# Halved second expert product in steps 5 to 15 of a fused attention and expert kernel

## The chip, the cores and the metric

The kernel runs on one core of a Trainium2 chip. The metric is the device time of one execution in microseconds. A core has TensorE (matrix products into PSUM; the trace calls its matmuls PE and its weight loads PEld), VectorE (DVE), ScalarE (ACT), GpSimd (POOL), and SyncE (SP), whose queue issues all DMA transfers of this kernel. Each engine works through its own queue in order and waits there for what its next instruction needs.

## The reference

The reference is chunked attention over 4 sequences of 768 tokens with 8 heads of 64, whose output x (3072 tokens by 512) goes through four experts, every token through all of them:

```
p = domain_probs / (domain_probs.sum(-1) + 1e-9)
for e in range(4):
    h = maximum(x @ w1[e], 0)          # 512 -> 1024
    out += p[:, e:e+1] * (h @ w2[e])   # 1024 -> 512
```

All inputs and the output are float32.

## The kernel before

**Precision.** Every operand of a large product is split into a high part and a low part (each of the type fp32r); a product is hi x hi + hi x lo + lo x hi, three matmuls accumulated in PSUM. `two_parts` (L306 ScalarE copy, L307 subtraction) makes such a pair; `split` (L344, L348) does it for single blocks of w1 and w2.

**Steps.** The expert part is a sequence of 16 steps n = 0 to 15: batch n // 4 (768 tokens, two halves of SG = 384), expert n % 4. Step 0 is computed plainly in the first block with attention of the first batch. From step 1 on, the first product (x @ w1) is done by seven products of half matrices in place of eight. Its blocks of w1 come in 4 pairs (block p and p + 4); per pair the sums S1 to S4 of weight blocks are formed, and the class `Pair` runs the seven products, 42 matmuls of 384 columns (`product`, L511), with results combined through PSUM and a small tile u (L524 copy, L528 addition) and then `relu` (L449, L450). The input side needs sums too, which `combine_x` makes once per batch (L317 to L326) into xa, xb and xc.

**Second product.** `Second` computes one tile of 128 tokens by 512 columns: 8 blocks of w2, three matmuls of 512 columns each (L482), 24 per tile, six tiles per step. The result times the routing weight is added into an SBUF tile acc (L496; L494 for the first expert), and stored after the fourth expert (L498). The very last tile is done as two halves of 256 columns.

**Weights.** In steps 1 to 4, `prep_pair` makes the w1 sums for a pair on POOL (L397 to L400) in the scratch tile s_t, of which there is one, splits them into four tiles of w1pool (8 buffers, two pairs) with L306/L307, and stores those in DRAM (`keep`, L359). In steps 0 to 3, `prep2` loads w2 blocks into the tile raw (3 buffers), splits them into w2pool (8 buffers) and stores them likewise. Later steps load the finished parts from DRAM (`again`, L363).

**Order.** TensorE's order is as written (`manual_schedule` for PE). The order on the other engines and on SP's queue is made by the planner of the framework, which plays the program through in a simulation and gives a buffer to the next ready user, by place in the program. Attention of later batches is spread over the steps in windows (`attend`), up to step 11: about two units of 96 queries per step.

**Last lines.** In step n, `tail`, the last tile of step n - 1, runs within pair 0 of step n; `next_pair` prepares pairs 2 and 3 of the step during pairs 1 and 2, and the first two pairs of step n + 1 during the second product.

Of the kernel before, what the change touches and what calls it, by code (L numbers as in the profile page):

```python
# [59 lines left out]
def tile_chunked_attention_moe(ctx: ExitStack, tc: tile.TileContext, qk, v, probs, w1, w2, out):  # L60
# [6 lines left out]
    raw = ctx.enter_context(tc.tile_pool(name="raw", bufs=3))  # L67
    w1pool = ctx.enter_context(tc.tile_pool(name="w1pool", bufs=8))
    w2pool = ctx.enter_context(tc.tile_pool(name="w2pool", bufs=8))
    hpool = ctx.enter_context(tc.tile_pool(name="hpool", bufs=NF * 2))  # L70
    opool = ctx.enter_context(tc.tile_pool(name="opool", bufs=6))
    dram = ctx.enter_context(tc.tile_pool(name="dram", bufs=1, space=DRAM))
# [7 lines left out]
    def open_late():  # L80
        head_ctx.close()
        late["sb"] = ctx.enter_context(tc.tile_pool(name="late", bufs=1, reuse_waits="tile"))
        late["s"] = ctx.enter_context(tc.tile_pool(name="ps_s", bufs=1, space=PSUM))
        late["a"] = ctx.enter_context(tc.tile_pool(name="ps_a", bufs=2, space=PSUM))
        late["xc"] = tuple(
            late["sb"].tile([P, 6, SG], F32R, name=f"xc_{part}", bufs=1) for part in ("hi", "lo")
        )

    idle = const.tile([P, P], mybir.dt.bfloat16, name="idle")
# [13 lines left out]
    ident = const.tile([P, P], F32, name="ident")  # L103
# [153 lines left out]
    def mix(u):  # L257
# [17 lines left out]
    xa, xb = (  # L275
        tuple(const.tile([P, NC, SG], F32R, name=f"{name}_{part}") for part in ("hi", "lo"))
        for name in ("xa", "xb")
# [31 lines left out]
    def combine_x(first):  # L309
# [4 lines left out]
        xc_hi, xc_lo = late["xc"]  # L314
        t3 = late["sb"].tile([P, NC, 256], F32, name="s_t").rearrange("p a b -> p (a b)")[:, 0:h2 * SG]
        t3 = t3.rearrange("p (a b) -> p a b", a=h2)
# [22 lines left out]
    def split(which, n, f):  # L339
# [7 lines left out]
        def low(eng):  # L347
            eng.tensor_tensor(out=lo, in0=r, in1=hi.bitcast(F32), op=ALU.subtract)  # L348
            if which == 2:
                keep(t, (2, n % E, f))  # L350
# [3 lines left out]

    kept = {}

    def keep(t, key, width=DM):
# [3 lines left out]
    def again(pool, name, key, width=DM):  # L361
        t = pool.tile([P, 2, DM], F32R, name=name)
        nc.sync.dma_start(t.bitcast(F32)[:, :, 0:width], kept[key])  # L363
        return t

    def prep2(n, f):
        if n >= E * B or (2, n, f) in wt:
            return
        if n < E:
            fetch(2, n, f)  # L370
            split(2, n, f)(nc.gpsimd)
        else:
            t = again(w2pool, "w2", (2, n % E, f))
            wt[2, n, f] = t[:, 0, :], t[:, 1, :]

# [9 lines left out]
    def prep_pair(n, p):  # L385

        if n >= E * B:
            return
        q = DM // 2
        if n > E:  # L390
            g = [again(w1pool, "w1", (1, n % E, p, i), DM if i < 3 else q) for i in range(4)]
        else:
            r = wp[n, p]
            a21, a22, a11, a12 = (r[:, i, :] for i in range(4))
            t = late["sb"].tile([P, 4, 256], F32, name="s_t")
            s4, s1, s2, s3 = (t[:, i, :] for i in range(4))
            nc.gpsimd.tensor_tensor(out=s1, in0=a21, in1=a22, op=ALU.add)  # L397
            nc.gpsimd.tensor_tensor(out=s2, in0=s1, in1=a11, op=ALU.subtract)
            nc.gpsimd.tensor_tensor(out=s4, in0=a12, in1=s2, op=ALU.subtract)
            nc.gpsimd.tensor_tensor(out=s3, in0=a11, in1=a21, op=ALU.subtract)  # L400
            g = [w1pool.tile([P, 2, DM], F32R, name="w1") for _ in range(4)]

            def put(i, lo, hi, x):
                two_parts(g[i][:, 0, lo:hi], g[i][:, 1, lo:hi], x, nc.vector)

            put(0, 0, DM, r[:, 2:4, :].rearrange("p a b -> p (a b)"))
            put(1, 0, q, a22)
# [356 lines left out]
```

## Time and profile before

| | |
|---|---|
| Time, median of 3 runs | 1114.11 us (1113.42 to 1116.62) |
| Profiled execution | 1114.95 us, span 1113.2 us |
| TensorE matmul busy | 1090.0 us, 6248 matmuls |
| VectorE, ScalarE, POOL busy | 589.6, 439.2, 161.8 us |
| Mean DMA rate | 204 GB/s over the span |
| Granted TensorE clock | 0.995 |

Rows of the profile read as follows. A group row names line, engine, operation, output <- inputs, shape and count, then after the bar busy time and mean ns of one, then idle time of the engine ahead of it and what ended that. A row of the timeline begins with start and duration in us; brackets hold the idle time before it and what ended it. The chain of waits follows the work that ended last. In the stage view each engine's busy time stands for a stretch of the span.

### The profile page before, as it was taken

To read this page: it belongs to the slowest core of one execution; us is meant where nothing else is said; L and a number is where in the kernel's file an instruction comes from. 1 tells how busy PE (TensorE), PEld (TensorE's weight loads), DVE (VectorE), ACT (ScalarE), POOL (GpSimd) and SP (SyncE) were. 2 spreads that over 40 slices of the span, in tenths; PEclk is the share of its full clock that TensorE was granted. 3 is DMA by queue.
4 is the path that set the end of the run, shared out by engine and by line. 5 is a ranking of instruction groups with operands and counts; after the bars stand their busy time and mean duration, and the time that the engine had idled before them with its cause. 6 is when DMAs were issued, how large, how long until landed. Compare 5 with 4: busy or idle time off the path is not lost.

```text
span 1113.2 us, 16383 instructions
## 1 busy us (share of the span) xinstructions
PE 1090.0 (98%) x6248; PEld 974.3 (88%) x6248; DVE 589.6 (53%) x1033; ACT 439.2 (39%) x919; POOL 161.8 (15%) x147
## 2 busy tenths in 40 slices
PE   7999999999999999999999999999999999999998
PEld 6888878988889898898989889898898989899897
DVE  6847985858775444445655534544474403233241
ACT  6555853637444343342523433332351313122130
POOL 4536531615241000000030000000012000000000
PEclk8999999999999999999999999999999999999999
DMA  7645882937379183571938538193652908264431
GB/s 241 226 149 201 321 311 95 403 147 287 146 273 348 62 319 124 216 251 66 338 107 302 182 136 297 62 335 108 241 201 107 338 29 328 88 260 155 163 122 57
DMA packets 87022, 226.57 MB, mean 204 GB/s; under 512 B 11552, under 2 KB 27168, under 8 KB 86944
## 3 DMA queue, kind: packets, MB, share of 16 engines
q1 hardware_dynamic: 86944, 225.53, 56.0%
q8 instruction: 49, 0.80, 0.3%
q14 instruction: 29, 0.24, 0.1%
HBM read 173.06 MB, written 52.43 MB: 203 GB/s over the span
## 4 chain that ended last, share of the span: by engine, by line
PE 84%; DVE 6%; issue 3%; ACT 2%; DMA 2%; POOL 2%; SPq 0%; DVEq 0%; ACTq 0%; POOLq 0%
PE moe_ps L482 43%; PE a_ps L511 20%; PE moe_ps L511 14%; PE moe_ps L439 2%; PE s_ps L147 2%; PE x_ps L263 2%; DMA k<-w 1%; DVE w L307 1%; DVE band L208 1%; ACT s_sb L164 1%; DVE aT L252 1%; DVE u L528 0%; ACT w L306 0%; DVE sm L195 0%; DVE s_sb L187 0%
## 5 line engine op out<-in xcount | busy, mean ns | idle before, releaser
L482 PE MATMUL moe_ps<-w,h_hi 128*128 128x512 f32 (+1 forms) x1552 | 478.8, 390 | 1.1 <-DVE h_lo L450 1.1
L482 PEld LDWEIGHTS moe_ps<-w,h_hi 128*128 128x128 f32 x1552 | 287.8, 188 | 60.3 <-DVE h_lo L450 1.4
L482 PE MATMUL moe_ps<-w,h_lo 128*128 128x512 f32 (+1 forms) x776 | 301.5, 389 | 0.0
L482 PEld LDWEIGHTS moe_ps<-w,h_lo 128*128 128x128 f32 x776 | 145.7, 188 | 30.0
L449 ACT ACTIVATE h_hi<-u 128x384 fp32r<-128x384 f32 x180 | 94.5, 525 | 173.5 <-DVE u L528 173.4
L496 DVE SCALAR_TENSOR_TENSOR acc<-moe_ps,pr,acc 128x512 f32<-128x512 f32 (+1 forms) x73 | 54.2, 742 | 156.3 <-PE moe_ps L482 155.7
L450 DVE SCALAR_TENSOR_TENSOR h_lo<-u,h_hi 128x384 fp32r<-128x384 f32 x180 | 106.9, 595 | 44.3 <-ACT h_hi L449 39.8
L528 DVE TENSOR_TENSOR u<-moe_ps,u 128x384 f32<-128x384 f32 x120 | 66.8, 556 | 106.2 <-PE moe_ps L511 105.7
L511 PE MATMUL a_ps<-xc_hi,w 128*128 128x384 f32 x480 | 104.6, 339 | 2.7 <-ACT u L524 2.0
L524 ACT COPY u<-a_ps 128x384 f32<-128x384 f32 x120 | 57.4, 478 | 106.0 <-PE a_ps L511 103.6
L511 PEld LDWEIGHTS a_ps<-xc_hi,w 128*128 128x128 f32 x480 | 86.3, 189 | 6.6 <-ACT u L524 3.5
L252 DVE STREAM_TRANSPOSE aT<-band 32x256 f32<-32x256 f32 x192 | 83.3, 434 | 10.2 <-ACT band L217 7.9
L164 ACT COPY s_sb<-s_ps 96x64 f32<-96x64 f32 (+1 forms) x96 | 39.6, 438 | 81.4 <-PE s_ps L147 80.8
L511 PE MATMUL a_ps<-xc_lo,w 128*128 128x384 f32 x240 | 61.6, 337 | 0.0
L450 DVE SCALAR_TENSOR_TENSOR h_lo<-a_ps,h_hi 128x384 fp32r<-128x384 f32 x60 | 33.1, 552 | 53.0 <-ACT h_hi L449 53.0
L511 PE MATMUL a_ps<-xb_hi,w 128*128 128x384 f32 x240 | 53.0, 343 | 5.6 <-DVE u L528 5.5
L348 POOL TENSOR_TENSOR w<-raw,w 128x512 fp32r<-128x512 f32 x31 | 43.8, 1422 | 82.1 <-ACT w L344 79.4
L528 DVE TENSOR_TENSOR u<-a_ps,u 128x384 f32<-128x384 f32 x60 | 33.4, 556 | 40.8 <-PE a_ps L511 23.3
L175 POOL MEMSET s_sb<- 32x64 f32 x4 | 0.6, 145 | 364.0 <-DVE acc L496 364.0
L511 PE MATMUL a_ps<-xa_hi,w 128*128 128x384 f32 x240 | 52.6, 341 | 0.3 <-DVE h_lo L450 0.3
L511 PE MATMUL moe_ps<-xb_hi,w 128*128 128x384 f32 x240 | 52.0, 339 | 0.0
L511 PE MATMUL moe_ps<-xa_hi,w 128*128 128x384 f32 x240 | 51.9, 338 | 0.0
(114 smaller groups left out, 1424.7 us busy)
## 6 DMA issues: line engine op xcount, KB each, us to landing
w<-k SPq DMA_DIRECT2D x228, 512.0 KB, 6.2
k<-w SPq DMA_DIRECT2D x80, 512.0 KB, 5.6
w<-k SPq DMA_DIRECT2D x44, 256.0 KB, 4.8
qk_t<-in_qk_dram SPq DMA_DIRECT2D x24, 448.0 KB, 3.5
raw<-in_w_dram SPq DMA_DIRECT2D x32, 256.0 KB, 5.1
v_t<-in_v_dram SPq DMA_DIRECT2D x32, 256.0 KB, 3.3
raw_pair<-in_w_dram SPq DMA_DIRECT2D x32, 256.0 KB, 4.7
out_dram<-acc SPq DMA_DIRECT2D x23, 256.0 KB, 2.0
```

The source lines that it names most:

```text
L147: nc.tensor.matmul(s_ps[0:UQ, j * NPAIR + g, :], lhsT=st[u]["qk"][rows, g * UQ:(g + 1) * UQ], rhs=st[u]["qk"][rows, NPAIR * UQ + g * P:NPA ...
L164: nc.scalar.copy(s_sb[rows, :, dst], s_ps[rows, :, src])
L252: nc.vector.transpose(out=aT[kb * CH:(kb + 1) * CH, :, c * CH:(c + 1) * CH], in_=band[c * CH:(c + 1) * CH, :, kb * CH:(kb + 1) * CH],)
L263: nc.tensor.matmul(x_ps[j * D:(j + 1) * D, g, :], lhsT=v_t[:, h * D:(h + 1) * D], rhs=aT[:, j * NPAIR + g, :], start=True, stop=True,)
L348: eng.tensor_tensor(out=lo, in0=r, in1=hi.bitcast(F32), op=ALU.subtract)
L449: last["act"] = nc.scalar.activation(h_hi[:, lo:hi], ps[:, lo:hi], AF.Relu)
L450: last["dve"] = nc.vector.scalar_tensor_tensor(out=h_lo[:, lo:hi], in0=ps[:, lo:hi], scalar=0.0, in1=h_hi.bitcast(F32)[:, lo:hi], op0=ALU. ...
L482: nc.tensor.matmul(self.ps, lhsT=h[:, self.rows], rhs=w[:, cols], start=(i == 0 and k == 0), stop=(i == NF - 1 and k == 2),)
L496: nc.vector.scalar_tensor_tensor(out=o, in0=self.ps, scalar=p_e, in1=o, op0=ALU.mult, op1=ALU.add)
L511: nc.tensor.matmul(ps, lhsT=w[:, c * P:(c + 1) * P], rhs=y[:, k0 + c, :], start=(first and i == 0), stop=(i == len(steps) - 1), skip_group ...
L524: nc.scalar.copy(u, ps)
L528: nc.vector.tensor_tensor(out=u, in0=ps, in1=u, op=ALU.add)
```

## The change

From step 5 to step 15 the second product too is done by seven products of halves: the hidden values h are split into halves by tokens (384) and by hidden columns (512), w2 by hidden rows (512) and output columns (256). Each of the seven products takes, for each of three token tiles, 4 blocks times 3 matmuls of 256 columns. Results accumulate in the two column halves of a PSUM bank per token tile and are added into acc after every product.

The weight sums T1 to T4 are made once per expert in steps 1 to 4 by the new function `prep2_combined`, called after each pair's `prep2`, from the raw blocks p and p + 4 (in step 4, expert 0, they are fetched again). It uses s_t and a new tile t_hi with one buffer, and stores four pieces of 256 KB per call. From step 5 all weights come from DRAM through one ring of 8 buffers (`Stream`), in the order of use. The sums of hidden values are made on POOL or VectorE and split (`Full.sums`, `split`). The pools of steps 1 to 4 are closed before step 5 and a new pool takes their place; xc moves to the constant pool, idle and ident to the pool of the first block, and the DMA scratch size is halved.

```diff
+    def open_fin():
+        mid_ctx.close()
+        late["sb"] = late["fin"] = ctx.enter_context(tc.tile_pool(name="fin", bufs=1, reuse_waits="tile"))
...
+    def prep2_combined(n, p):
+
+        e, q = n % E, DM // 2
+        if n >= E:
+            for f in (p, p + NH):
+                fetch(2, n + E * B, f)
+                raws[n, f] = wt[2, n + E * B, f]
+        r0, r1 = raws[n, p], raws[n, p + NH]
+        b11, b12, b21, b22 = r0[:, 0:q], r0[:, q:], r1[:, 0:q], r1[:, q:]
+        t = late["sb"].tile([P, 4, 256], F32, name="s_t")
+        t1, t2, t3, t4 = (t[:, i, :] for i in range(4))
+        nc.gpsimd.tensor_tensor(out=t1, in0=b12, in1=b11, op=ALU.subtract)
+        nc.gpsimd.tensor_tensor(out=t2, in0=t1, in1=b22, op=ALU.subtract)
+        nc.gpsimd.tensor_tensor(out=t4, in0=b21, in1=t2, op=ALU.add)
+        nc.gpsimd.tensor_tensor(out=t3, in0=b22, in1=b12, op=ALU.subtract)
+        for i in range(2):
+            x = t[:, 2 * i:2 * i + 2, :].rearrange("p a b -> p (a b)")
+            hi = late["sb"].tile([P, DM], F32R, name="t_hi")
+            nc.scalar.copy(hi, x)
+            (nc.gpsimd, nc.vector)[i].tensor_tensor(
+                out=x.bitcast(F32R), in0=x, in1=hi.bitcast(F32), op=ALU.subtract
+            )
+            k = kept2("t2", e, i)
+            nc.sync.dma_start(k[:, p, 0], hi.bitcast(F32))
+            nc.sync.dma_start(k[:, p, 1], x)
...
+    class Stream:
...
+        def send(self):
+            q = DM // 2
+            while self.sent < min(len(self.keys), self.free + self.RING):
+                key = n, which, x, i = self.keys[self.sent]
+                t = late["fin"].tile([P, 2 * DM], F32R, name="ring", bufs=self.RING)
...
+                    src = kept2(kind, n % E, half)[:, 2 * i:2 * i + 2, :, o * q:(o + 1) * q]
+                nc.sync.dma_start(dst.bitcast(F32), src)
...
+        def sums(self):
+
+            eng = nc.vector if self.p == NP2 - 1 else nc.gpsimd
+            s1, s2 = self.new("s1"), self.new("s2")
+            eng.tensor_tensor(out=s1, in0=self.u22, in1=self.u21, op=ALU.add)
+            eng.tensor_tensor(out=s2, in0=self.u11, in1=s1, op=ALU.subtract)
+            self.split("S2", s2)
+            self.split("S1", s1)
+            nc.gpsimd.tensor_tensor(out=self.u21, in0=self.u11, in1=self.u21, op=ALU.subtract)
+            self.split("S3", self.u21)
+            nc.gpsimd.tensor_tensor(out=self.u12, in0=self.u12, in1=s2, op=ALU.add)
+            self.split("S4", self.u12)
...
+        def go(self, name, t):
+            left, right = self.WITH[name]
...
+            for k in range(NP2):
+                w = self.stream.at[self.n, 2, right, k // 2][:, k % 2]
+                hi, lo = self.k[k][left]
+                for i, (x, y) in enumerate(((hi, 0), (hi, 1), (lo, 0))):
+                    nc.tensor.matmul(
+                        ps, lhsT=x[:, rows], rhs=w[:, y, :],
+                        start=(begins and k == 0 and i == 0), stop=(k == NP2 - 1 and i == 2),
...
+                nc.vector.scalar_tensor_tensor(out=o, in0=ps, scalar=p_e, in1=o, op0=ALU.mult, op1=ALU.add)
...
-        for n in range(1, B * E):
+        for n in range(1, E + 1):
...
             for f in KORDER[0:2]:
                 prep2(n, f)
+            prep2_combined(n, 0)
             pair.seven()
...
                 for f in KORDER[2 * p:2 * p + 2]:
                     prep2(n, f)
+                prep2_combined(n, p)
                 if p + 1 < NP2:
                     next_pair(n, p + 1)
...
         tail.go()
+        open_fin()
+        us, i = windows[E + 1, "A"]
+        load_qk(us[i])
+
+        stream = Stream(range(E + 1, B * E))
...
+            second.go("1", 0)
+            pair.four()
+            pair.three()
+            pair.sums()
+            second.go("1", 1)
+            second.go("2", 0)
+            second.go("2", 1)
+            second.go("1", 2)
+            second.go("2", 2)
...
+            for name in "65":
+                for t in range(NTT):
+                    second.go(name, t)
+            attend(n, "B")
+            for name, t in (("7", 2), ("7", 0), ("7", 1), ("4", 2), ("4", 0), ("4", 1), ("3", 0), ("3", 2)):
+                second.go(name, t)
...
-    nc = _bacc.Bacc("TRN2", target_bir_lowering=False, num_devices=1, dynamic_dma_scratch_size=1024)
+    nc = _bacc.Bacc("TRN2", target_bir_lowering=False, num_devices=1, dynamic_dma_scratch_size=512)
```

More of the change, by code (lines that the diff above doesn't have):

```diff
@@ L385, in prep_pair @@
     def prep_pair(n, p):
[L387 removed]
+        if n > E:
             return
         q = DM // 2
[L390 to L407, printed above, removed]
[L408 to L412 removed]
@@ L631, in window @@
             scores(u)
-            if u + 1 < len(units):
+            if not last and u + 1 < len(units):
                 load_qk(u + 1)
```

238 lines of the change are left out of this document (201 added, 37 removed).

## The prediction

> **What bounds the kernel now.** I read the page first, for the share of each engine.
>
> ```profile
> span 1113.2 us, 16383 instructions
> ...
> PE 1090.0 (98%) x6248; PEld 974.3 (88%) x6248; DVE 589.6 (53%) x1033; ACT 439.2 (39%) x919; POOL 161.8 (15%) x147
> ```
>
> TensorE is busy nearly all the time and sets the end. The profiled execution took 1114.95 us, of which 1113.2 us are the span; the sum is made against 1114.95, which is 0.84 us above the median of the three timed runs. Then the chain of waits in order of time (start, duration, what), at some marks. L482 x18 begins where the first product of a step ends.
>
> ```profile
> 217.53 4.12 PE moe_ps L482 x18
> 355.88 4.12 PE moe_ps L482 x18
> 1012.52 4.12 PE moe_ps L482 x18
> 1018.73 23.16 PE moe_ps L482 x102
> 1066.38 2.11 PE a_ps L511 x12
> 1074.79 4.12 PE moe_ps L482 x18
> ```
>
> A late step without attention takes 1074.79 - 1012.52 = 62.27 us. A 512-column matmul costs 23.16 / 102 = 227 ns, a 384-column one 2.11 / 12 = 176 ns; 168 x 0.176 + 144 x 0.227 = 62.3 us, so the late steps are pure TensorE, with nothing in between. There a shorter product is worth its full time.
>
> **The product itself.** The changed steps run 7 x 3 x 12 = 252 matmuls of 256 columns in place of 144 of 512. The last output tile of the kernel before is computed in two halves of 256 columns, so the price is in the trace: TensorE in order of time near the end, where each such row is followed by one h_lo matmul; below them the group of their weight loads, for later.
>
> ```profile
> 1104.00 0.40 PE L482 MATMUL moe_ps<-w,h_hi 128*128 128x256 f32 x2
> ...
> 1108.67 0.40 PE L482 MATMUL moe_ps<-w,h_hi 128*128 128x256 f32 x2
> ...
> L482 PEld LDWEIGHTS moe_ps<-w,h_hi 128*128 128x128 f32 x1552 | 287.8, 188 | 60.3 <-DVE h_lo L450 1.4
> ```
>
> Thirteen groups of three in 4.67 us are 120 ns per matmul. 252 x 0.120 = 30.2 us against 144 x 0.227 = 32.7 us: 2.4 us less per step, 11 steps: **-26.4 us**. [...]
>
> **What the changed steps need beside TensorE.** First the weights. Per step the ring brings 7.34 MB for each product, 14.7 MB in about 60 us: 246 GB/s. The second product's pieces have runs of 1 KB. Two stretches of the DMA view, one with packets of 4 KB alone, one (2 us at 474) with mostly 1 KB packets by number, and the page's landing time of the stored weights:
>
> ```profile
> DMA packets 567, 2.06 MB, mean 413 GB/s; under 512 B 63, under 2 KB 63, under 8 KB 567
> DMA packets 410, 0.78 MB, mean 390 GB/s; under 512 B 29, under 2 KB 283, under 8 KB 410
> ...
> w<-k SPq DMA_DIRECT2D x228, 512.0 KB, 6.2
> ```
>
> In the second, about 127 packets of 4 KB account for 127 x 4 KB x 16 / 413 GB/s = 20 us of the 32 engine-us; the 254 of 1 KB share 12 us, 47 ns each, about 345 GB/s. So 7.34 / 0.413 + 7.34 / 0.345 = 39 us of transfer hide in a step of 60. A ring slot is reloaded at least one pair (42 x 0.176 = 7.4 us of TensorE) before its use, against 6.2 us: hidden, with little to spare.
>
> Then VectorE and ScalarE. Stage view over one step's length with two attention units and over one without (columns: stretch, length, PE, PEld, DVE, ACT and POOL busy, clock, DMA share, GB/s), and the prices of the new small operations:
>
> ```profile
> 422.28:488.68 66.40, 66.40 (x377) 59.55 (x377) 32.53 (x62) 22.65 (x49) 0.00 (x0) 1.00 0.55 196
> 950.26:1012.52 62.26, 62.26 (x313) 56.48 (x313) 19.54 (x34) 13.49 (x29) 0.00 (x0) 1.00 0.52 185
> L496 DVE SCALAR_TENSOR_TENSOR acc<-moe_ps,pr,acc 128x256 f32<-128x256 f32 x2 | 1.0, 485 | 4.5 <-PE moe_ps L482 4.5
> L528 DVE TENSOR_TENSOR u<-moe_ps,u 128x384 f32<-128x384 f32 x120 | 66.8, 556 | 106.2 <-PE moe_ps L511 105.7
> ```
>
> VectorE per step: 21 evictions x 0.485, and 42 operations of 384 columns (12 adds, 28 low parts, two sums) x 0.556, together 33.5 us in place of 19.5. Two attention units add 32.5 - 19.5 = 13 us: 46.5 of 64 us. The steps that also combine the inputs of the next batch (7 and 11) are fuller still. TensorE waits only where an eviction comes late; the shortest cover is one piece of 12 matmuls, 1.44 us, against 0.485. I put 3 us on all eleven steps (below: 0; above: 10, if step 7 and 11 queue up). ScalarE rises to about 40 of 64 us, POOL to 15. The end: one eviction and one 256 KB store in place of halves, +0.3 us.
>
> **The preparation in steps 1 to 4** is where I expect the time to go. The T weights are made by a new function, 16 calls, 4 per step. A call takes the scratch tile s_t, of which there is one, and the new tile t_hi, also one. s_t is today used by the preparation of the first product's weights (prep_pair, L397 to L400). POOL and DVE in order of time show how it is passed on:
>
> ```profile
> 126.44 0.74 POOL L397 TENSOR_TENSOR s_t<-raw_pair 128x256 f32<-128x256 f32 x1 [1.95 <-issue]
> 157.16 0.73 POOL L397 TENSOR_TENSOR s_t<-raw_pair 128x256 f32<-128x256 f32 x1 [3.31 <-issue]
> 197.31 1.04 DVE L307 TENSOR_TENSOR w<-s_t,w 128x256 fp32r<-128x256 f32 x1
> 198.49 0.94 POOL L397 TENSOR_TENSOR s_t<-raw_pair 128x256 f32<-128x256 f32 x1 [0.41 <-POOL w L348]
> 206.76 0.74 POOL L397 TENSOR_TENSOR s_t<-raw_pair 128x256 f32<-128x256 f32 x1 [3.56 <-issue]
> 315.52 0.73 POOL L397 TENSOR_TENSOR s_t<-raw_pair 128x256 f32<-128x256 f32 x1 [3.76 <-DVE w L307]
> 319.76 0.74 POOL L397 TENSOR_TENSOR s_t<-raw_pair 128x256 f32<-128x256 f32 x1 [1.31 <-DVE w L307]
> ```
>
> The next use starts 0.14 us after the last reader ends (198.35 to 198.49): s_t is always in somebody's hands, partly because a preparation waits, holding it, for weight buffers (157 to 198). The preparations of pairs 2 and 3 run about 8 us ahead of the TensorE that uses them: the one at 198.49 is for pair 3 of step 2, whose S2 is needed 4.2 us before 217.53. There is no slack for more. An unhindered hold is 319.76 - 315.52 = 4.2 us, with queues 8.3 (198.49 to 206.76); I take 6.5.
>
> One call of the new function holds s_t until its last store has left it, and between its two halves t_hi must be stored too: two POOL operations, ScalarE copy, store, ScalarE copy, VectorE subtraction, store. Prices: POOL from the view of s_t, the rest from the groups by shape.
>
> ```profile
> L398 POOL TENSOR_TENSOR s_t<-s_t,raw_pair x16: 727/740/1202, 82.2 to 338.7; 128x256 f32<-128x256 f32 x16
> L344 ACT CAST w<-raw 128x512 fp32r<-128x512 f32 x32 | 19.7, 618 | 5.8 <-DMA raw<-in_w_dram 5.2
> L307 DVE TENSOR_TENSOR w<-s_t,w 128x512 fp32r<-128x512 f32 x16 | 13.7, 858 | 2.9 <-ACT w L306 2.9
> ```
>
> 2 x 0.74 + 2 x 0.62 + 0.86 = 3.6 us, five handovers of 0.15 and half a us of queueing (an estimate): 4.8 us, plus two stores of 256 KB. How long these take depends on the load. The stage view with POOL alone (length, POOL, clock, DMA share, GB/s), the landing times of 256 KB in 186 to 228 and in 409 to 475, and on the page:
>
> ```profile
> 150.00:186.00 36.00, 7.46 (x8) 1.00 0.38 137
> 186.00:228.00 42.00, 25.41 (x24) 1.00 0.94 365
> ...
> raw<-in_w_dram SPq DMA_DIRECT2D x8, 256.0 KB, 5.0
> ...
> v_t<-in_v_dram SPq DMA_DIRECT2D x2, 256.0 KB, 3.2
> ...
> out_dram<-acc SPq DMA_DIRECT2D x23, 256.0 KB, 2.0
> ```
>
> The DMA engines are already full in the first product of step 2, just where calls fall; the change adds 16 stores of 256 KB, 4.2 MB, to each of the four steps. A store lies between 2.0 us (quiet) and 5.0 (full). I take 3.6, the middle, since a step that grows longer has less load per us. One call is then c = 4.8 + 2 x 3.6 = **12 us**; bounds 8.8 and 14.8. [...]
>
> Now the chain of s_t. The calls stand before the preparations of pairs 2 and 3 in the program, so I expect the planner to serve them first when both are ready. From 126 us, where the fourth preparation starts, to the end of the last one lie 13 preparations (84 us), 15 calls (15c), one combination of inputs (8 us), and about 8 us in which a preparation waits for weight buffers: 126 + 84 + 15c + 16. The S2 part of the last is ready 2.5 us before its end, and TensorE wants it at 355.88 - 4.2 = 351.7. The stall over steps 1 to 4 is 15c - 128, nothing below c = 8.5: **+52 us** at c = 12. Late behind it are the raw tiles of w2 (three buffers, now held through the call), and whatever SP queues behind a store that waits.
>
> Other edits at nothing: the unchanged first product's matmuls, moved pools and scratch size; the ring's first loads, whose buffers are free from the middle of step 4, 30 us before use. Sum: 1114.95 - 26.4 + 3 + 0.3 + 52 = 1143.9, **1143 us** beside the median.
>
> **Rivals.** (1) The scratch tile is hidden: the calls go into the quiet stretches (150 to 186: DMA share 0.38, POOL 7.5 of 36 us) and the stores take 2 us, c at or under 8.5. For it: seven tenths of the DMA time there is free; against: s_t is held by a waiting preparation in just these stretches. Time 1114.1 - 26.4 + 3.3 = 1091. (2) Stores at the full load's 5.0 us: c = 14.8, stall 94, 1185. Against: once TensorE stalls, the load thins out. (3) The stall equals the gain at c = 10.1; 0.2 us of c is 3 us, so no change is a narrow case. (4) The halves do not go faster since a weight load (188 ns in its group) bounds a short matmul: 252 x 0.188 = 47 us per step, +160 us; the 120 ns row speaks against it, 1 in 50. (5) VectorE or the ring bounds the changed steps: 2.4 us of each is given back, near 1114 with the preparation hidden; the bounds above leave it unlikely.
>
> **How the numbers follow.** Chain as summed, c from 10.3 to 14.8, that is 1118 to 1185: 0.50, with the likeliest near 1143. Beyond: 0.07. Hidden or half hidden (1087 to 1110): 0.37. Between, within 0.3% (3.3 us, about what a measurement of this kernel can tell from no change): 0.06. The range to 8 in 10 takes both signs, 1087 to 1187; the likeliest case alone spans 1118 to 1185. Faster 0.37, same 0.06, slower 0.57.
>
> **What would show it.** The period of the last steps should be near 59.8 us, with 120 ns per matmul of 256. The first x18-like mark of step 4 (355.88 now) should come some 50 us later, with TensorE waiting for L306/L307 parts of s_t and stores from s_t and t_hi of 3 to 4 us. The prediction is wrong if step 4's first product ends near 356 us, if the holds of s_t by the new function are under 9 us, or if the planner serves pairs 2 and 3 first and TensorE never waits for them.

## The result and the profile after

The changed kernel takes 1215.62 us (median of 4 runs, 1213.58 to 1216.68) against 1114.42 us of the kernel before beside it: a ratio of 1.0903, 95% interval 1.0881 to 1.0925, 101 us slower. The forecast was 29 us slower; the time lies above the whole range.

The page of the kernel after, its span and engines:

```profile
span 1214.2 us, 19938 instructions
PE 1088.4 (90%) x7412; PEld 1023.6 (84%) x7412; DVE 783.3 (65%) x1355; ACT 595.0 (49%) x1271; POOL 403.3 (33%) x381
```

TensorE is as long busy as before (1088 against 1090 us); what was added to the span is waiting. The waits of TensorE, after (waiting product and line, what it waited for, us in total, times, longest):

```profile
PE a_ps L553 <- ACT w L308: 57.4, 8, 11.8
PE a_ps L553 <- ACT u L674: 36.8, 22, 4.8
```

Two waits hold nearly all of it, one in each part of the kernel. L308 is the split of the w1 sums out of s_t in steps 1 to 4 (L306 before). L674 is in the new code of steps 5 to 15. The chain of waits, after, at the ends of the first products of steps 1, 2 and 4, and for steps 14 and 15 at the same place of each (some 36 matmuls into the second product):

```profile
164.00 4.12 PE moe_ps L524 x18
250.18 4.12 PE moe_ps L524 x18
427.45 4.12 PE moe_ps L524 x18
...
1119.54 4.70 PE moe_ps L757 x37
1183.55 4.70 PE moe_ps L757 x37
```

The mark of step 4 is 427.45 where it was 355.88: **71.6 us were lost in steps 1 to 4**. From there to the end of the span it is 786.8 us where it was 757.3: **29.4 us were lost in steps 5 to 15**, where the forecast had a gain of 23. Together 101.

The stage view, TensorE alone, for both stretches (stretch, length, busy time and matmuls, granted clock, DMA share, GB/s), first after, then before:

```profile
109.00:427.00 318.00, 254.02 (x1369) 0.90 0.70 251
427.45:1214.20 786.75, 735.11 (x5272) 0.99 0.69 226
```

```profile
109.00:356.00 247.00, 239.60 (x1360) 0.99 0.69 259
355.88:1113.00 757.12, 752.89 (x4108) 1.00 0.52 185
```

In steps 1 to 4 TensorE's idle time rose from 7.4 to 64.0 us (+56.6), and nearly the same matmuls took 14.4 us longer, at a clock of 0.90 in place of 0.99. In steps 5 to 15 the product did its part, with TensorE 17.8 us less busy, and the idle time rose from 4.2 to 51.6 us (+47.4). These four numbers, +56.6, +14.4, -17.8 and +47.4, add up to the 101 us.

**Steps 1 to 4: who holds s_t.** GpSimd in order of time, after. L401 is the first operation of a T call on a new s_t, L402 needs the second raw block, L434 is the first operation of a w1 preparation; in brackets the idle time before:

```profile
104.61 1.12 POOL L401 TENSOR_TENSOR s_t<-raw 128x256 f32<-128x256 f32 x1 [2.23 <-DVE w L309]
114.39 0.90 POOL L401 TENSOR_TENSOR s_t<-raw 128x256 f32<-128x256 f32 x1 [4.64 <-DMA t<-s_t]
122.10 0.74 POOL L402 TENSOR_TENSOR s_t<-s_t,raw 128x256 f32<-128x256 f32 x1 [1.46 <-DMA raw<-in_w_dram]
135.11 0.72 POOL L434 TENSOR_TENSOR s_t<-raw_pair 128x256 f32<-128x256 f32 x1 [2.67 <-DMA t<-s_t]
...
195.07 0.74 POOL L401 TENSOR_TENSOR s_t<-raw 128x256 f32<-128x256 f32 x1 [4.48 <-DVE s_sb L189]
209.62 0.74 POOL L402 TENSOR_TENSOR s_t<-s_t,raw 128x256 f32<-128x256 f32 x1 [4.24 <-DMA raw<-in_w_dram]
222.60 0.72 POOL L434 TENSOR_TENSOR s_t<-raw_pair 128x256 f32<-128x256 f32 x1 [2.58 <-DVE h_lo L492]
227.75 0.73 POOL L401 TENSOR_TENSOR s_t<-raw 128x256 f32<-128x256 f32 x1 [2.26 <-DVE w L309]
241.52 0.72 POOL L434 TENSOR_TENSOR s_t<-raw_pair 128x256 f32<-128x256 f32 x1 [4.22 <-DMA t<-s_t]
```

From a T call to the next user of the tile: 104.61 to 114.39 is 9.8 us, 227.75 to 241.52 is 13.8. But 114.39 to 135.11 is 20.7 and 195.07 to 222.60 is 27.5: these two calls took the tile with one of their two raw blocks there, and held it while the other was still to come from memory (L402 at 122.10 and 209.62). The preparation of the next pair waits behind that, and TensorE behind the preparation.

After the block had come, two splits of w2 (L353) still ran on GpSimd among the operations of each of these calls, 3.1 us at 123.50 and 125.67. Another call, in step 4, held the tile for 21.7 us (369.59 to 391.27) with both blocks there: its last store was issued at 382.02 and landed 9.1 us later, at a DMA share of 0.99. Of the fifteen holds that GpSimd's timeline shows, four are longer than 20 us, one in each step; the other eleven lie between 8.8 and 14.4.

The end of one wait of TensorE for such a preparation, TensorE in order of time, after, and the stage view round it:

```profile
157.43 1.73 PE L553 MATMUL a_ps<-xc_hi,w 128*128 128x384 f32 x4 [9.39 <-ACT w L308]
...
162.79 0.86 PE L553 MATMUL a_ps<-xc_hi,w 128*128 128x384 f32 x4
```

```profile
155.00:165.00 10.00, 7.57 (x30) 0.65 0.64 229
```

After a wait of 9.39 us the same four matmuls take 1.73 us in place of 0.86, and full rate is back 5.4 us later at the latest; at 160.88, 3.5 us after the wait, two matmuls still took 0.84 us where they take 0.51 at full rate. The granted clock of this stretch is 0.65. The 14.4 us of longer matmuls lie in such stretches: taken in slices of 10 us, every slice of steps 1 to 4 with a clock under 0.95 has one of the eight waits for L308 in it or just ahead of it. After the short waits of the next section, 1.4 to 1.5 us, four such matmuls took 0.96 us.

**Steps 5 to 15: who holds u11.** In each changed step a small tile takes the first result of a pair:

```
def new(self, name):
    return late["fin"].tile([P, SG], F32, name=name, bufs=2)
...
self.u11 = self.new("u11")
nc.scalar.copy(self.u11, self.a)                                       # L674
...
eng = nc.vector if self.p == NP2 - 1 else nc.gpsimd
...
eng.tensor_tensor(out=s1, in0=self.u22, in1=self.u21, op=ALU.add)       # L716
eng.tensor_tensor(out=s2, in0=self.u11, in1=s1, op=ALU.subtract)       # L717
...
nc.gpsimd.tensor_tensor(out=self.u21, in0=self.u11, in1=self.u21, ...) # L720
...
nc.gpsimd.tensor_tensor(out=self.u12, in0=self.u12, in1=s2, ...)       # L722
```

There are two u11, so the third pair's copy needs the first pair's to be read out. GpSimd, ScalarE and TensorE in order of time in a late step, after:

```profile
1159.35 1.02 POOL L716 TENSOR_TENSOR s<-u,u 128x384 f32<-128x384 f32 x1 [35.20 <-ACT u L659]
1160.44 1.01 POOL L717 TENSOR_TENSOR s<-u,s 128x384 f32<-128x384 f32 x1
1161.42 1.32 POOL L720 TENSOR_TENSOR u<-u,u 128x384 f32<-128x384 f32 x1
```

```profile
1163.19 0.47 ACT L674 COPY u<-a_ps 128x384 f32<-128x384 f32 x1
```

```profile
1159.69 0.51 PE L553 MATMUL a_ps<-xa_lo,ring 128*128 128x384 f32 x2
...
1163.71 0.96 PE L553 MATMUL a_ps<-xc_hi,ring 128*128 128x384 f32 x4 [1.43 <-ACT u L674]
```

The product that L674 copies ended near 1160.2. The copy starts at 1163.19, after L720, the last reader of the old u11, has ended at 1162.74; the next product of the pair that adds into the same PSUM bank (`six`) waits for it. GpSimd has been idle for 35 us before, until ScalarE's L659 gave it its input: it is not full, it is late. This happens twice in each step, 22 times in eleven.

### The profile page after: what moved, and what is told of

It reads as the page before. It is cut to its first block, busy times and chain, and to the rows that moved or that the text cites. A ratio compares the mean times of both kernels' runs of the same rounds, so it can differ in the third digit from the quotient of the medians.

```text
span 1214.2 us, 19938 instructions
## 1 busy us (share of the span) xinstructions
PE 1088.4 (90%) x7412; PEld 1023.6 (84%) x7412; DVE 783.3 (65%) x1355; ACT 595.0 (49%) x1271; POOL 403.3 (33%) x381
## 4 chain that ended last, share of the span: by engine, by line
PE 66%; DVE 12%; POOL 7%; DMA 6%; ACT 6%; issue 3%; SPq 0%; POOLq 0%; DVEq 0%; ACTq 0%
PE a_ps L553 16%; PE a_ps L757 13%; PE moe_ps L553 12%; PE moe_ps L757 10%; PE moe_ps L524 9%; DMA t<-s_t 2%; PE moe_ps L481 2%; DVE S_lo L309 2%; DMA raw<-in_w_dram 2%; PE x_ps L265 2%; DVE aT L254 2%; DMA t<-t_hi 2%; DVE acc L774 1%; DVE A_lo L309 1%; PE s_ps L149 1%
## 5 line engine op out<-in xcount | busy, mean ns | idle before, releaser
L716 POOL TENSOR_TENSOR s<-u,u 128x384 f32<-128x384 f32 x33 | 33.5, 1014 | 499.0 <-ACT u L659 499.0
L524 PE MATMUL moe_ps<-w,h_hi 128*128 128x512 f32 x480 | 150.6, 393 | 1.1 <-DVE h_lo L492 1.1
L757 PE MATMUL a_ps<-ring,S_hi 128*128 128x256 f32 x704 | 130.1, 284 | 0.0
L659 ACT ACTIVATE u<-u 128x384 f32<-128x384 f32 x132 | 69.1, 525 | 102.5 <-DVE u L677 39.2
L309 DVE TENSOR_TENSOR A_lo<-u,A_hi 128x384 fp32r<-128x384 f32 x132 | 85.3, 653 | 45.9 <-ACT A_hi L308 45.9
L553 PE MATMUL a_ps<-xc_hi,ring 128*128 128x384 f32 x352 | 79.1, 347 | 36.8 <-ACT u L674 36.8
L757 PEld LDWEIGHTS a_ps<-ring,S_hi 128*128 128x128 f32 x704 | 109.9, 191 | 1.8 <-DVE acc L774 0.8
L524 PEld LDWEIGHTS moe_ps<-w,h_hi 128*128 128x128 f32 x480 | 89.1, 188 | 20.2 <-DVE h_lo L492 1.4
L309 DVE TENSOR_TENSOR S_lo<-s,S_hi 128x384 fp32r<-128x384 f32 x88 | 100.8, 1171 | 0.0
L757 PE MATMUL a_ps<-ring,S_lo 128*128 128x256 f32 x352 | 99.5, 283 | 0.0
L524 PE MATMUL moe_ps<-w,h_lo 128*128 128x512 f32 x240 | 93.9, 391 | 0.0
L553 PE MATMUL a_ps<-xc_hi,w 128*128 128x384 f32 x128 | 35.1, 402 | 62.7 <-ACT w L308 57.4
L757 PE MATMUL moe_ps<-ring,A_hi 128*128 128x256 f32 x440 | 80.4, 283 | 0.0
L720 POOL TENSOR_TENSOR u<-u,u 128x384 f32<-128x384 f32 x44 | 57.9, 1315 | 32.9 <-DVE s L716 32.9
```

The source lines that it names most:

```text
L309: eng.tensor_tensor(out=lo, in0=x, in1=hi.bitcast(F32), op=ALU.subtract)
L524: nc.tensor.matmul(self.ps, lhsT=h[:, self.rows], rhs=w[:, cols], start=(i == 0 and k == 0), stop=(i == NF - 1 and k == 2),)
L553: nc.tensor.matmul(ps, lhsT=w[:, c * P:(c + 1) * P], rhs=y[:, k0 + c, :], start=(first and i == 0), stop=(i == len(steps) - 1), skip_group ...
L659: nc.scalar.activation(x, x, AF.Relu)
L716: eng.tensor_tensor(out=s1, in0=self.u22, in1=self.u21, op=ALU.add)
L720: nc.gpsimd.tensor_tensor(out=self.u21, in0=self.u11, in1=self.u21, op=ALU.subtract)
```

## The experiments

The marks below are those of the two parts: the first product's end in step 4 (427.45 in the change, 355.88 before) and the time from it to the end of the span (786.8 and 757.3).

### The two parts alone: without T, and T alone

First T is left out of steps 1 to 4, and the ring reads quarters of w2 of the same size in its place; the output is then not the reference's, and only the time is of use.

```diff
-                  "T1": ("t2", 0, 0), "T2": ("t2", 0, 1), "T3": ("t2", 1, 0), "T4": ("t2", 1, 1)}
+                  "T1": ("w2", 0, 0), "T2": ("w2", 0, 1), "T3": ("w2", 1, 0), "T4": ("w2", 1, 1)}
...
-            prep2_combined(n, 0)
...
-                prep2_combined(n, p)
```

> Leaves out the making of T1 to T4 in steps 1 to 4 altogether; the ring reads quarters of w2 of the same size in their place, so the result is not the reference's. Theory (one scratch tile s_t, passed between the two preparations, is what delays steps 1 to 4): the first product of step 4 ends near 356 us as in the kernel before (427 with the change), and the time falls by about 72 us, to 1143. Rival (the steps from 5 on take their own time whatever comes before, and part of the 72 us is slack that they eat): the mark falls by 72 us, the time by clearly less.

Measured: 1145.38 us (1143.92 to 1150.03), ratio 1.029, interval 1.0265 to 1.0316. The mark is 361.19, the rest 786.8 us, the same as in the change. The profile is of the longest of the four executions (1150.03), 4.7 us above their median, so the 5.3 us that its mark lies above 355.88 are not counted as a loss; the other run without T, below, has its mark at 356.82.

The other half: T made as in the change, and steps 5 to 15 as before.

```diff
-        for n in range(1, E + 1):
+        for n in range(1, B * E):
...
-            prep2_combined(n, 0)
+            if n <= E:
+                prep2_combined(n, 0)
...
-        open_fin()
...
-        stream = Stream(range(E + 1, B * E))
...
-        for n in range(E + 1, B * E):
...
+        mid_ctx.close()
```

> T1 to T4 are made and stored in steps 1 to 4 exactly as in the change, but steps 5 to 15 run the second product as before (T is never used). Theory: with the part from step 5 on at +29 us as measured without T, this part alone is +72: 1186, the first product of step 4 ending near 427 us. Rival (part of the delay of steps 1 to 4 comes from the closing of the pools for the later steps): 1114 to 1160.

Measured: 1188.36 us (1186.55 to 1189.94), ratio 1.0659, interval 1.0643 to 1.0675; mark 429.07, rest 756.8 us. Its waits of TensorE:

```profile
PE a_ps L561 <- ACT w L308: 57.6, 8, 11.4
```

What follows: making T costs 74 us by itself, and the changed steps are 31 us slower than the old ones by themselves; 105 us added up, 101 measured together. The losses are nearly separate, and the eleven steps lose even where T costs nothing.

### Steps 5 to 15: a third u11, then the sums on VectorE

```diff
-            self.u11 = self.new("u11")
+            self.u11 = late["fin"].tile([P, SG], F32, name="u11", bufs=3)
...
-    nc = _bacc.Bacc("TRN2", target_bir_lowering=False, num_devices=1, dynamic_dma_scratch_size=512)
+    nc = _bacc.Bacc("TRN2", target_bir_lowering=False, num_devices=1, dynamic_dma_scratch_size=256)
```

> The change with a third buffer for the tile u11 (the DMA scratch size goes from 512 to 256 to make room). Theory (from step 5 on, TensorE's sixth product waits for the copy of A11, and that copy waits for a free u11, which the POOL sums of the pair two back still read): the 22 waits of 1.4 us and more on ScalarE's copy at L674 vanish, 36.8 us and about 0.2 us of slow matmuls after each, so 1215.6 - 41 = 1175. Rival (ScalarE's queue is simply too full there): the wait stays, 1205 to 1216.

Measured: 1201.78 us (1199.67 to 1203.35), ratio 1.0788, interval 1.0772 to 1.0804; 14 us less than the change, where the theory had 41. Its waits of TensorE:

```profile
PE a_ps L553 <- ACT w L308: 55.4, 8, 10.4
PE a_ps L553 <- ACT u L684: 20.0, 20, 5.5
```

The wait for L674 is gone, and L684, the copy into u21 of the same pair, took its place with half of the time: u21 too has two buffers and is read by the same L716 and L720. A buffer more for one tile moved the wait to the next.

So the lateness itself was taken away: s1 and s2 of every pair on VectorE, beside the third u11. This run also has the in-place form of T of the next section, whose own run is its comparison.

```diff
-            eng = nc.vector if self.p == NP2 - 1 else nc.gpsimd
+            eng = nc.vector
```

> As the run with T in place and three u11, with the sums s1 and s2 of all four pairs on VectorE (before: pairs 0 to 2 on POOL). Theory (the 20 waits on the copy at L684 are a tile u21 that the POOL sums of two pairs back still hold): the sums end 2 us earlier, the waits vanish and with them about 20 us: 1150. Rival (VectorE is the tighter engine, and 66 more operations on it cost more than POOL's lateness): 1165 to 1180.

Measured: 1159.55 us (1157.38 to 1159.98), ratio 1.0397, interval 1.0381 to 1.0412, 11 us less than the same kernel with the sums on GpSimd (1170.78); rest 761.6 against 774.4 us. The theory had 1150. Of 20 waits for u21 two are left. The chain of waits in the last steps and the waits of TensorE:

```profile
1005.49 4.70 PE moe_ps L754 x37
1066.46 4.70 PE moe_ps L754 x37
```

```profile
PE a_ps L550 <- ACT u L681: 10.3, 2, 5.1
```

A late step now takes 60.97 us, against 64.01 in the change and 62.27 before: here the seven products do pay, 1.3 us a step. The two waits left, 5 us each, are in steps 7 and 11, where VectorE also makes the inputs of the next batch with operations of 128x1536 and 128x768.

Both late edits together without T, the ring reading quarters of w2 as in the first run, to ask whether the change could have paid at all:

```diff
-            self.u11 = self.new("u11")
+            self.u11 = late["fin"].tile([P, SG], F32, name="u11", bufs=3)
...
-            eng = nc.vector if self.p == NP2 - 1 else nc.gpsimd
+            eng = nc.vector
...
-            prep2_combined(n, 0)
...
-                prep2_combined(n, p)
```

> The change with the making of T left out of steps 1 to 4 (the ring reads quarters of w2 in its place, so the output is not the reference's), and in steps 5 to 15 three buffers for u11 and all of s1 and s2 on VectorE. It asks what the seven products are worth when T costs nothing and the tiles of the sums are free in time. Theory, that both losses only add: 1145.4 us of the run without T, less the 25.2 us that the two edits took out of steps 5 to 15 (786.8 to 761.6 us): 1120 us, still above the kernel before, since TensorE's idle time in those steps is then about 27 us against 4. Rival: without T's work in front of them the steps gain more, and the product's 18 to 26 us show: 1090 to 1105 us.

Measured: 1119.61 us (1118.01 to 1122.89), ratio 1.0045, interval 1.0027 to 1.0064. The stage view from the mark of step 4 to the end:

```profile
356.82:1117.80 760.98, 733.43 (x5273) 0.99 0.70 233
```

The chain of waits at the marks of steps 6 and 9:

```profile
495.71 4.69 PE moe_ps L757 x37
700.17 4.69 PE moe_ps L757 x37
```

The losses only add. With T free and the tiles in time, TensorE is busy 19.5 us less than before in these steps (733.4 against 752.9) and idle 23.3 us more (27.6 against 4.2): still slower than the kernel before, by 5 us. The marks say where. A late step is 1.3 us shorter than before, and steps 6 and 10, with two units of attention each, are 1.0 us shorter (65.4 against 66.4). From the mark of step 6 to that of step 9 it is 204.5 us against 199.9 before, and from step 10 to step 13 199.7 against 195.3. In the form tried, what the product gains elsewhere does not pay for what these two stretches lose, where steps 7 and 11 make the inputs of the next batch.

### Steps 1 to 4: which resource sets the stall

T made in place in the raw tiles, so that s_t isn't used, with the third u11:

```diff
-        t = late["sb"].tile([P, 4, 256], F32, name="s_t")
-        t1, t2, t3, t4 = (t[:, i, :] for i in range(4))
-        nc.gpsimd.tensor_tensor(out=t1, in0=b12, in1=b11, op=ALU.subtract)
...
+        nc.gpsimd.tensor_tensor(out=b11, in0=b12, in1=b11, op=ALU.subtract)
+        nc.gpsimd.tensor_tensor(out=b12, in0=b22, in1=b12, op=ALU.subtract)
+        nc.gpsimd.tensor_tensor(out=b22, in0=b11, in1=b22, op=ALU.subtract)
+        nc.gpsimd.tensor_tensor(out=b21, in0=b21, in1=b22, op=ALU.add)
...
```

> T1 to T4 are made in place in the raw tiles of w2, no longer in s_t, and stored from there; same operations, same stores, same t_hi; u11 has three buffers too. Theory: steps 1 to 4 lose their 72 us (unless the three raw tiles, now held longer, bind: then 10 to 30 us of it stay), so 1102 to 1130. Rival (the added POOL, ScalarE and DMA work itself delays steps 1 to 4, whatever tile it uses): 1160 or more.

Measured: 1170.78 us (1170.05 to 1174.81), ratio 1.052, interval 1.0495 to 1.0544, 31 us less than with the third u11 alone. The mark is 394.67. Its waits of TensorE:

```profile
PE a_ps L550 <- ACT u L681: 19.5, 20, 5.5
PE moe_ps L521 <- ACT w L349: 18.8, 5, 10.0
PE moe_ps L521 <- POOL w L353: 8.5, 7, 4.4
```

The wait for L308 is gone from the top: s_t was the cause of it. The stall fell from 72 to 39 us and no further. TensorE now waits for the splits of w2 (L349, L353), and SP's queue waited 16.3 us, 10 times, with the fetch of a raw block for a store out of a raw tile, a wait that the change does not have, since it stores out of s_t: the three raw tiles are now held through the stores. The time lies in the rival's range all the same (1160 or more: the added work itself delays these steps, whatever tile it uses), so this run alone does not part the tiles from the work. The runs with late calls below do the same work elsewhere, with the raw blocks fetched again, and leave 17 us of the stall.

Two edits on the change itself left the parts in place. The first swaps two lines, the preparation of the next pair ahead of the T call:

```diff
-                prep2_combined(n, p)
                 if p + 1 < NP2:
                     next_pair(n, p + 1)
+                prep2_combined(n, p)
```

> The change with two lines swapped: in pairs 1 to 3 the first product's preparation of the next pair stands ahead of the T call in the program. Nothing else. If the order in which the planner gives out s_t sets the stall: the preparations of pairs 2 and 3 no longer stand behind two T calls, and 20 to 40 of the 72 us go, 1175 to 1195. If the total of the holds sets it (s_t is handed on without a gap, whoever is first): 1205 to 1218.

Measured: 1202.70 us (1200.55 to 1203.50), ratio 1.0786, interval 1.0768 to 1.0804; mark 411.62, 16 us earlier. The wait for L308 is 35.8 us over 5 times. The time lies between the two cases expected. The order is worth a fifth of the stall, with the four longest holds at 16.2 to 22.3 us in place of 20.7 to 27.5; the rest stays. A second s_t was not tried.

The second gives t_hi two buffers:

```diff
-            hi = late["sb"].tile([P, DM], F32R, name="t_hi")
+            hi = late["sb"].tile([P, DM], F32R, name="t_hi", bufs=2)
...
-            u = late["sb"].tile([P, SG], F32, name="u", bufs=4)
+            u = late["sb"].tile([P, SG], F32, name="u", bufs=3)
...
-    nc = _bacc.Bacc("TRN2", target_bir_lowering=False, num_devices=1, dynamic_dma_scratch_size=512)
+    nc = _bacc.Bacc("TRN2", target_bir_lowering=False, num_devices=1, dynamic_dma_scratch_size=256)
```

> The change with two buffers for t_hi (paid for by three instead of four u buffers and by half the DMA scratch). If the stall of steps 1 to 4 is 15 holds of the scratch tile (a hold ends with the last store of it), a call no longer waits for the store of the first high part before the second is made: about 3 us less per hold, 15 x 3 = 45 us less, some 1172 us, with the mark of step 4 near 385. Rival: the hold is set by the wait for raw blocks and by the store of s_t itself, which stay: less than 15 us, 1200 to 1216 us; a third: the fewer u buffers cost more than that in steps 5 to 15, which the time from the mark of step 4 to the end would show (786.8 us in the change).

Measured: 1200.95 us (1197.45 to 1203.71), ratio 1.0762, interval 1.0724 to 1.0801; mark 410.04, 17 us earlier, rest 788.7. GpSimd in order of time in this kernel:

```profile
189.27 0.73 POOL L401 TENSOR_TENSOR s_t<-raw 128x256 f32<-128x256 f32 x1 [4.52 <-DMA t<-s_t]
204.96 0.74 POOL L402 TENSOR_TENSOR s_t<-s_t,raw 128x256 f32<-128x256 f32 x1 [2.74 <-DMA raw<-in_w_dram]
216.12 0.72 POOL L434 TENSOR_TENSOR s_t<-raw_pair 128x256 f32<-128x256 f32 x1 [0.72 <-DMA t<-s_t]
221.59 0.73 POOL L401 TENSOR_TENSOR s_t<-raw 128x256 f32<-128x256 f32 x1 [2.26 <-DVE w L309]
...
232.76 0.72 POOL L434 TENSOR_TENSOR s_t<-raw_pair 128x256 f32<-128x256 f32 x1 [1.34 <-DMA t<-s_t]
```

The last call shown holds s_t for 11.2 us, where the same call held it 13.8 us in the change. The one before it, which waits for its second block, holds it 26.9 us (27.5 in the change). Fifteen times 2.6 us would have been 39. Over all fifteen holds it is 17.0 us (226.9 to 209.9), and the mark comes 17.4 us earlier: the stall follows the sum of the holds, but the mean hold fell by 1.1 us and not by 3. The work of most calls got shorter, the waits for raw blocks inside the hold did not. The theory (45 us) is refuted; the time, 14.7 us less, lies just within the first rival (under 15, the hold set by raw blocks and by the store of s_t). The third rival, the fewer u buffers, costs 2 us at most.

Then the calls were moved out of the first product, on top of the in-place form with the sums on VectorE. The raw blocks are fetched again and the four calls of a step made among its second products:

```diff
-        if n >= E:
-            for f in (p, p + NH):
...
+        for f in (p, p + NH):
...
-            prep2_combined(n, 0)
...
+            prep2_combined(n, 0)
+            prep2_combined(n, 1)
...
             attend(n, "B")
...
+            prep2_combined(n, 2)
+            prep2_combined(n, 3)
```

> As the run before (T in place, three u11, sums on VectorE), but the raw blocks for T are fetched a second time, and the T calls stand in the second product's part of each step, so that the raw tiles of prep2 are free as early as in the kernel before. Theory: the remaining 39 us of steps 1 to 4 (raw tiles held through a call, so that w2's splits come late) go to under 10: about 1115 to 1120. Rival (the DMA and POOL work of T itself delays the steps, wherever it stands): 1140 or more.

Measured: 1156.90 us (1151.96 to 1158.26), ratio 1.0369, interval 1.0344 to 1.0394. The mark is 372.65, 24 us earlier than in the kernel it builds on (396.48), so the loss in steps 1 to 4 is down to 17 us; but one wait of 19.7 us, for the ring's first load, takes most of it back, and the time stays in the rival's range (1140 or more). I thought step 4's late calls held the old pools open, and put those back into the first product:

```diff
-            prep2_combined(n, 0)
+            if n == E:
+                prep2_combined(n, 0)
...
+            if n < E:
+                prep2_combined(n, 0)
+                prep2_combined(n, 1)
```

> Same as the run before it with late T calls, but step 4 makes its T in its first product, where the change had it, so that the old pools close in time. If the one 19.7 us wait for the ring's first load came from step 4's late T calls, it and the slow matmuls behind it go: about 1157 - 20 = 1137 us, the range 1132 to 1142. Rival: step 4's T calls, with no raw tiles of their own fetched again in time, delay its first product by as much as they did in steps 1 to 4 of the earlier form (about 6 us a step by 24 over 4) and hold the ring's first load all the same: 1143 to 1157 us.

Measured: 1156.82 us (1156.46 to 1158.42), ratio 1.037, interval 1.0346 to 1.0395: no change, as the rival had it. Its waits of TensorE, and GpSimd's first operation of each T call in place (L399) in order of time:

```profile
PE a_ps L549 <- DMA ring<-k: 20.1, 1, 20.1
PE a_ps L549 <- ACT u L680: 10.7, 2, 5.3
```

```profile
376.89 0.74 POOL L399 TENSOR_TENSOR raw<-raw 128x256 f32<-128x256 f32 x1 [8.82 <-DMA raw<-in_w_dram]
391.29 0.74 POOL L399 TENSOR_TENSOR raw<-raw 128x256 f32<-128x256 f32 x1 [7.58 <-DMA raw<-in_w_dram]
...
411.25 0.73 POOL L399 TENSOR_TENSOR raw<-raw 128x256 f32<-128x256 f32 x1 [6.14 <-DMA raw<-in_w_dram]
419.62 0.72 POOL L399 TENSOR_TENSOR raw<-raw 128x256 f32<-128x256 f32 x1 [4.14 <-DMA raw<-in_w_dram]
```

The calls follow each other 8.4 to 14.4 us apart, each waiting for raw blocks; SP's queue waited 26.9 us, 18 times, with the fetch of a raw block for a store out of a raw tile. The last call begins at 419.62, 47 us after the mark; in the run before it began at 419.58, so the place in the program made no difference. The chain of holds has moved from s_t to the raw tiles. SP's queue issues the last store of the last call at 424.56 and the ring's first load at 427.07. That the load waits for these calls also follows from the order of the pools; no run took that wait away.

Last, on top of that run, two of the long VectorE operations that make the inputs of the next batch, put on GpSimd:

```diff
-            two_parts(xa[0], xa[1], xr[:, 0], nc.vector)
-            two_parts(xb[0][:, h2:NC], xb[1][:, h2:NC], b22, nc.vector)
+            two_parts(xa[0], xa[1], xr[:, 0], nc.gpsimd)
+            two_parts(xb[0][:, h2:NC], xb[1][:, h2:NC], b22, nc.gpsimd)
```

> As the run beside it, and in steps 7 and 11 the low parts of the combined inputs (two of the four long operations of 2.1 us) are made by GpSimd instead of VectorE. Theory: each of these steps is some 74 us against 61 to 62 of its neighbours of the same build because VectorE's long operations delay the evictions; with half of them gone each loses about 6 us: 12 us less than the run beside it, about 1125 us. Rival: GpSimd is late with them and the first matmuls of those steps wait for the inputs instead, or VectorE slows down beside it: no change or up to 10 us more.

Measured: 1170.93 us (1169.62 to 1174.88), ratio 1.05, interval 1.0469 to 1.0531, 14 us more than the run that it builds on (1156.82), where the theory had 12 less. Its waits of TensorE have the ones of steps 7 and 11 doubled:

```profile
PE a_ps L549 <- ACT u L680: 18.9, 2, 9.5
```

GpSimd took 3.5 us for the longest of them against 2.3 on VectorE. The two waits are 8.2 us longer together, which matches the time from the mark to the end, 789.9 against 782.3 us. The mark itself came 5.4 us later (378.06 against 372.70): the edited lines also run in step 3, which makes the inputs of the second batch, and GpSimd has the same long operation there, at 294.02. That this makes the 5.4 us is likely, not shown.

## Why the prediction was wrong, step by step

The sign was right, and T in steps 1 to 4 was named as the main loss. Two steps failed, and the larger one was a step costed near nothing. Against the forecast the product gave 8.6 us less, the waits of steps 5 to 15 cost 44.4 us more and the stall of steps 1 to 4 19.6 us more; together 72.6, the distance from 1143 to 1215.6.

- **The product, -26.4 us.** The price held: 24 matmuls of 256 columns take 2.88 us in the chain after (120 ns), so the rival with a weight load as bound is refuted. A late step's TensorE time fell from 62.27 to 60.39 us (busy time from 1119.54 to 1183.55), not to 59.8; over all eleven steps busy time fell by 17.8 us. Mis-sized by 8.6; where the 8.6 us go is not shown.
- **"I put 3 us on all eleven steps."** This is the step that failed: the idle time of these steps rose by 47.4 us. The engines' loads were nearly as forecast. Stage view of a late step, after (columns as in the prediction's):

```profile
1119.54:1183.55 64.01, 60.39 (x420) 59.35 (x420) 37.48 (x64) 25.91 (x57) 16.08 (x14) 1.00 0.70 231
```

  VectorE 37.5 us against 33.5, GpSimd 16 against 15. VectorE's low parts (L309) make up the difference: 29 of them took 20.8 us in this step, where the forecast's 0.556 us each gives 16.1. But the argument went by load and by the length of an eviction, 0.485 us under a cover of 1.44 us. What counts is when the tile that the eviction writes into is free. GpSimd's sums end some 2.5 us after the copy wanted u11, and a load of a quarter of the step says nothing of that. The two-buffer tiles of `Full.new` were not followed from their last reader to their next writer. No rival named it; the third u11 and the sums on VectorE showed it (786.8 to 774.0 and 761.6 us).
- **The upper bound of that term, "10, if step 7 and 11 queue up",** had the right place: these steps keep two waits of 5 us when u11 has three buffers and the sums are on VectorE.
- **The stall of steps 1 to 4, +52 us.** The resource and the wait were right: s_t, with TensorE waiting for L308, 57.4 us; T in place took that wait away. Measured 71.6 us: 56.6 of idle time and 14.4 of matmuls at a lower clock after the waits; the sum had stalls as idle time alone. The term that was mis-sized is c. The fifteen holds have a mean of 15.1 us, above the upper bound of 14.8. Eleven have a mean of 11.9, the c = 12 of the forecast; three waited inside the hold for a raw block, up to 27.5 us, which the sum did not have, and one for a late store. By the sum's own 15c - 128 that is a stall of 99 us. Only 72 came, since the thirteen preparations and the combination of inputs, with their waits, took 85 us in place of 100 and the first three calls, 43.7 us of holds, put off the fourth preparation by 28.2 us only (from 126.44 to 154.65). That the idle time of 56.6 us is close to 52 is luck. The slope, one us of stall for each us by which the holds grow together, did show: 17.0 us less of holds with the second t_hi, 17.4 us less of stall.
- **The stores, 3.6 us each.** The landing times of the stores of s_t, least, median and most, were 2.0, 2.7 and 9.1 us: lower in the middle than taken, with a long tail. The store that took 9.1 us, at a DMA share of 0.99, is the one of step 4's long hold. At 2.0 us for all of them c is 8.8 and the sum's 15c - 128 a stall of 4 us, and that did not come.
- **Raw tiles "late behind it".** Named, not priced. Where s_t was taken out of the way a stall of 39 us was left, most of it at the splits out of these tiles (18.8 and 8.5 us of waits).
- **The ring.** Hidden, as costed: 231 GB/s in the late step against 246, pieces landing in 4.4 to 5.2 us, and no wait of TensorE for it in the change. Its first loads cost nothing there, and nothing in the two runs without T; with T's calls late, close ahead of step 5, they cost 20 us.
- **Rivals.** Hidden T (1091): refuted by T alone, +74 us. Full-load stores (1185): the stall was between the two, the stores were not that slow (median 2.7 us). The 3.3 us that the likeliest case put on steps 5 to 15 and the end were carried into both, so neither could reach 1216. The rival in which the changed steps are bound by something other than TensorE had the right place, but named VectorE and the ring, and allowed for no more than the product's gain.

## What to carry to other kernels

An engine that is 25% busy can still be the bound (GpSimd here, 16.1 of 64.0 us in a late step): for each tile that a new step writes, follow its last reader to its next writer, with the number of buffers, before costing the step by engine load. A scratch tile with one buffer is priced by the longest thing that its holder may wait for while holding it, not by the holder's own work (the longest hold of s_t was 27.5 us, where eleven of fifteen had a mean of 11.9); give the holder all of its inputs first (not tried here), or expect the wait to move to the next scarce tile when this one is freed. A stall of several us on TensorE cost more than its length here: after a wait of 9.39 us four matmuls took 1.73 us in place of 0.86, and nearly the same matmuls of steps 1 to 4 took 14.4 us longer in all.

## What was not expected of the hardware

- After a wait of 9.39 us TensorE ran at half rate (1.73 against 0.86 us for four matmuls of 384 columns) and was back at full rate 5.4 us later at the latest. After waits of 1.4 to 1.5 us the same four matmuls took 0.96 us; after one of 2.64 us (377.95) 0.96 as well, after one of 3.33 us (138.41) 1.73.
- VectorE's subtractions of the same size took different times. The low parts of s1 and s2 took 1171 ns, those of S3 and S4 545. In the late step above the low parts of one pair's s1 and s2, from 1161.80 on and beside GpSimd's L720 and L722 (1161.42 to 1164.01), took 2.63 us together; that of its S3 at 1164.35, with GpSimd idle, took 0.55. Groups of VectorE by line, after, and then in the kernel with s1 and s2 on VectorE:

```profile
L309 DVE TENSOR_TENSOR S_lo<-s,S_hi 128x384 fp32r<-128x384 f32 x88 | 100.8, 1171 | 0.0
...
L309 DVE TENSOR_TENSOR S_lo<-u,S_hi 128x384 fp32r<-128x384 f32 x88 | 47.8, 545 | 0.0
```

```profile
L309 DVE TENSOR_TENSOR S_lo<-s,S_hi 128x384 fp32r<-128x384 f32 x88 | 77.5, 883 | 0.0
```

  With two of the four sums off GpSimd the same operation fell to 883 ns. What makes it longer no run here shows.
